# Two attentions and a gated MLP in one kernel: the fourfold pooled sum of the stacked head pairs is split between ScalarE and VectorE, the fp32 v loads get a third buffer, and the written order of all steps is drawn anew

## The chip, the core and the metric

The kernel runs on one core of one Trainium2 chip. The core has a matrix engine (TensorE, PE in the profile, with its weight loads as PEld), VectorE (DVE), ScalarE (ACT), GpSimd (POOL) and SyncE (SP), which only issues transfers; 16 DMA engines move data. Each engine has its own queue of instructions and works it off in order; semaphores make it wait for the others. The metric is the device time of one execution in microseconds, as the median of several runs.

## What is computed

For q, k and v of 8 batches, 8 heads, 576 positions and 64 features, two attentions are added: one over keys and queries averaged in fours, whose result is repeated fourfold, and a local one, in which a position sees only those less than four away. The sum, laid out as 4608 tokens of 512 features, goes through a gated MLP.

```python
q_d = q.reshape(B, H, Sd, 4, D).mean(axis=3)          # k_d, v_d alike
out_up = np.repeat(sm_attn(q_d, k_d, v_d), 4, axis=2)
mask = np.abs(pos[:, None] - pos[None, :]) < 4
out_local = softmax(where(mask, scale * q @ k.T, -1e9)) @ v
x = (out_up + out_local).transpose(0, 2, 1, 3).reshape(4608, 512)
return (np.maximum(x @ w_gate, 0) * (x @ w_val)) @ w_out   # 512 -> 1536 -> 512
```

## The kernel before, in words

**Work and tiles.** The heads are taken two at a time, 32 pairs, and the tokens in nine chunks of 512. Each pair leaves its part of x, transposed (features on partitions), in `xT`. As soon as four pairs have filled the columns of a chunk, the chunk's MLP can run: `hg` and `hv` (L919) are its products with w_gate and w_val, `gate` the gated product on VectorE, and then follow the products with w_out. Many of the large products are computed by a scheme that needs seven half-sized products in place of eight (classes `Unit`, `Half7`, `Seven`; L1004, L1264, L1167), with additions on VectorE and copies out of PSUM on ScalarE (L1275, L1280, L1178, L1185).

**Pairs.** Pairs 0 to 11 go through an older form. For the first nine, q and k are turned by TensorE (`tr`, L540 and L556), taken out of PSUM by ScalarE and VectorE (`ev`, L576 and L579), scored (`s1`), exponentiated on ScalarE (`ex`, `ed`) and masked on VectorE (`ma`). v is pooled by TensorE (`vd`, L618) and copied out by ScalarE (`vc`). For the first four pairs `sd`, `su` and `xp` make the output and turn it into `xT`. Between them, `warm` and `brief` issue matmuls on zeros, whose results nobody reads.

Pairs 12 to 31 are "stacked": the two heads of a pair lie in the two halves of the partitions, and one step, `so` (`emit_section`, L852), interleaves the matmuls of three pairs' phases (scores of the next pair, denominators of this one, numerators of the last). ScalarE exponentiates (L858, L863) and makes the reciprocals as exp(-ln(x)) (L874, L877). VectorE multiplies (`xn`, L880) into one buffer, `xn`, of 576 local and 144 pooled columns. Then `xsum` (L886, VectorE) adds the local columns and the pooled ones, each of which it reads four times in a row by a step of zero, and writes the pair's 128x576 part of `xT`.

**v of the stacked pairs** comes twice. One load, in fp16 and by GpSimd's queue, serves the local attention (`v`). The other, in fp32 and by SyncE's queue, serves the pooled one (`v4`, `emit_load_v4`). GpSimd folds the latter's twelve rows in two steps: `v2` (L589) adds rows in twos from buffer `v4n[hp % 2]` into `v2full[hp % 2]`, and `v1` (L597) adds again into `vp[hp % 3]`, in fp16.

**Order.** All instructions stand in the order of the string `SEQ`, step by step; each engine gets its own instructions in that order. POOL issues the loads of q, k, v (L454, L459, L504, L477) and of the weights (L1076, L1082) and does the folds; SP issues the first q load, the transposes by DMA (`flip`), the fp32 v loads and the outputs. `SEQ` begins with `cast`, `ones/6`, `ones/4`, `ones/5` (L1504: three memsets of `vw` buffers on POOL) and `loadk/0`. Ahead of `SEQ` stand the first q load, three loads of constants and twelve wide filler matmuls.

Of the kernel before, what the change touches and what calls it, by code (L numbers as in the profile page):

```python
# [23 lines left out]
loadk/3 ev/2/01A/0 xp/0/0/4 ev/2/11A/2 ev/2/00A/0 xe/0/1V/5 s1/2/0 vc/1/6 sd/1/6 ma/1/1 rd/1/6 xe/0/0A/4 td/1/6 wv/0
wg/0 warm/3/7 su/1/4 loadk/4 ex/2/1/0 vd/2/6 ed/2/0 ex/2/0/0 tr/3/1/2 tr/3/2/3 vc/2/6 edge/1 wg/1 ru/1/4 tr/3/0/0
tu/1/0/4 tu/1/1/4 ev/3/21V/3 ev/3/11A/2 ev/3/10A/2 ev/3/01A/0 ev/3/00A/0 sd/2/6 xp/1/0/4 ev/3/20V/3 loadq/5 ma/2/0
xe/1/0A/4 xp/1/1/5 rd/2/6 s1/3/0 ma/2/1 loadk/5 ex/3/0/0 xe/1/1V/5 loadk/6 hv/0/0/7 loadv/4 su/2/4 td/2/6 ed/3/0
loadv/5 vd/3/6 ru/2/4 warm/4/1 tu/2/1/4 hv/1/0/1 ex/3/1/0 tu/2/0/4 tr/4/0/0 xp/2/0/4 ma/3/1 vc/3/6 ev/4/00A/0 loadq/6
# [5 lines left out]
hg/3/*/0 wo/2 wo/3 ev/5/10A/3 hg/2/*/6 den/4/1/5 gate/0/7 gate/1/1 den/4/0/4 relu/3/0 qk/b3/0@0 tr/6/1/0 relu/2/6
loadv/8 hv/2/*/7 vd/5/1 num/4/1/3 qk/a2/1@0 ln/4 gate/2/7 ev/6/10A/0 inv qk/b0/0@0 num/4/0/2 s1/5/4 vc/5/1 hv/3/*/1
xn/2 ex/5/0/4 hg/4/*/2 ed/5/4 ev/6/11V/0 xsum/4 qk/a0/1@0 gate/3/1 tr/7/1/0 tr/6/0/4 tr/6/2/1 qk/b2/0@0 ex/5/1/4
ma/5/1 ev/6/20V/1 hv/4/*/3 ev/7/10V/0 hg/5/*/6 ev/7/11V/0 ev/6/21V/1 relu/4/2 ev/6/00A/4 vd/6/1 ev/6/01V/4 den/5/1/5
ma/5/0 qk/b1/0@0 flip/9 vc/6/1 gate/4/3 den/5/0/4 ln/4 num/5/0/2 num/5/1/3 relu/5/6 hv/5/*/7 inv hg/7/*/1 qk/a1/1@0
gate/5/7 relu/7/1 v/a/1@0 s1/6/4 ed/6/4 xn/2 v/b/0@0 ex/6/1/4 hv/8/*/0 v4/b/1@0 ex/6/0/4 ma/6/1 qk/a3/1@0 qk/b0/1@0
hv/7/*/3 sum/2/0@1 hg/8/*/2 relu/8/2 hg/6/*/7 tr/7/2/1 ma/6/0 tr/7/0/6 relu/6/7 gate/7/3 den/6/0/4 ev/7/00A/6 gate/8/0  # L40
ev/7/21A/1 edge/0 ev/7/20A/1 den/6/1/5 num/6/1/3 v4/a/0@1 qk/b1/0@2 tr/8/2/0 ln/4 xsum/5 ev/7/01V/6 num/6/0/2 v2/b/0@1
qk/b3/1@0 qk/b2/1@0 ev/8/21A/0 inv hv/6/*/7 gate/6/7 hv/9/*/1 ev/8/20A/0 s1/7/4 ed/7/4 ex/7/1/4 qk/b1/0@1 ex/7/0/4
hg/9/*/0 relu/9/0 xn/2 hg/10/*/3 qk/a1/0@1 hg/11/*/7 flip/10 hv/10/*/6 zs/0.1/0@1 ma/7/1 vd/7/4 ma/7/0 hv/11/*/0
relu/10/3 den/7/1/5 gate/9/1 xsum/6 vc/7/4 tr/8/0/1 relu/11/7 p/1/0@1 wt/0 keep/1/0@1 gate/10/6 gate/11/0 ev/8/01A/1
num/7/0/6 den/7/0/4 next/0/1@0 qk/a3/0@1 ln/4 num/7/1/7 tr/8/1/0 sumhi/0/0@1 qk/b1/1@0 p/2/0@1 qk/b0/0@1 next/1/1@0
ev/8/00A/1 wt/1 p/5/0@1 inv ev/8/10A/0 sumhi/1/0@1 wt/2 ev/8/11A/0 xn/6 p/6/0@1 xsum/7 flip/11 v/b/1@0 keep/2/0@1
vd/8/5 wt/3 zs/0.0/0@1 vc/8/5 qk/b2/0@1 p/7/0@1 scores/a/0@1 hg/0/0@1 exp/a0/0@1 keep/3/0@1 ed/a/0@1 qk/a2/0@1
mask/a0/0@1 hv/0/0@1 p/4/0@1 qk/b3/0@1 qk/a0/0@1 exp/a1/0@1 o/a10/0@1 mask/a1/0@1 v2/a/1@1 relu/0/0@1 o/a00/0@1
sum/3/0@1 c22//0@1 c11//0@1 o/a01/0@1 c21//0@1 qk/a1/1@1 o/a11/0@1 hg/1/0@1 hg/2/0@1 ln/a/0@1 next/0/0@1 inv/a/0@1
v4/b/0@1 relu/1/0@1 const p/3/0@1 hg/3/0@1 relu/2/0@1 xn/a/0@1 v1/a/1@1 gate/0/0@1 c12//0@1 hv/2/0@1 xsum/a/0@1 vd/9/7  # L50
pool/b/0@1 qk/a0/1@1 hv/1/0@1 flip/12 relu/3/0@1 gate/2/0@1 vd/10/2 gate/1/0@1 vc/9/7 scores/b/0@1 hg/4/0@1 exp/b0/0@1
exp/b1/0@1 qk/b2/0@2 qk/a2/1@1 next/1/0@1 flip/13 hv/3/0@1 relu/4/0@1 ed/b/0@1 hv/4/0@1 vc/10/2 p/1/1@1 mask/b1/0@1
mask/b0/0@1 gate/3/0@1 pool/a/0@1 o/b01/0@1 tn/1/0@1 keep/1/1@1 o/b10/0@1 o/b00/0@1 gate/4/0@1 o/b11/0@1 zs/1.1/0@1
v/a/0@1 ln/b/0@1 p/6/1@1 v/b/0@1 qk/a3/1@1 inv/b/0@1 hg/5/0@1 qk/b1/1@1 xn/b/0@1 relu/5/0@1 hv/5/0@1 keep/2/1@1
next/2/0@1 scores/a/1@1 exp/a1/1@1 xsum/b/0@1 next/3/0@1 p/2/1@1 p/7/1@1 keep/3/1@1 flip/14 exp/a0/1@1 hg/0/1@1
ed/a/1@1 gate/5/0@1 hv/0/1@1 p/5/1@1 zs/3.1/0@1 mask/a1/1@1 qk/b0/1@1 o/a01/1@1 relu/0/1@1 mask/a0/1@1 o/a10/1@1
zs/1.0/0@1 o/a00/1@1 c11//1@1 o/a11/1@1 ln/a/1@1 inv/a/1@1 p/4/1@1 c22//1@1 qk/a1/1@2 p/3/1@1 c21//1@1 hg/2/1@1
pool/b/1@1 gate/0/1@1 c12//1@1 qk/b2/1@1 relu/2/1@1 xn/a/1@1 qk/b3/1@1 hv/2/1@1 gate/2/1@1 scores/b/1@1 hv/1/1@1
v/a/1@1 zs/2.1/0@1 exp/b0/1@1 exp/b1/1@1 mask/b0/1@1 hg/1/1@1 qk/a1/0@2 mask/b1/1@1 ed/b/1@1 xsum/a/1@1 o/b00/1@1
pool/a/1@1 o/b01/1@1 ln/b/1@1 relu/1/1@1 xq/0/0@2 gate/1/1@1 o/b10/1@1 inv/b/1@1 o/b11/1@1 v2/b/1@1 hg/4/1@1  # L60
so/b400/1@1 xn/b/1@1 hv/4/1@1 hg/3/1@1 qk/a0/0@2 pool/b/0@2 relu/4/1@1 gate/4/1@1 xsum/b/1@1 ed/a4/0@2 v4/b/1@1
hv/3/1@1 qk/a2/0@2 sq/4.23.0.1/0@2 exp/a4/0@2 relu/3/1@1 so/a460/0@2 sk/4.23.0.1/0@2 tn/3/0@1 v1/a/0@2 hg/5/1@1
v1/b/1@1 ln/a6/0@2 gate/3/1@1 next/0/1@1 relu/5/1@1 sq/4.23.0.5/0@2 sq/0.70.2.1/0@2 ed/b4/0@2 sq/4.23.0.2/0@2 flip/15
sum/2/0@2 zs/2.0/0@1 exp/b4/0@2 sk/4.23.0.5/0@2 hv/5/1@1 xq/1/0@2 vh/10.6/0@2 sk/0.70.2.1/0@2 sq/4.23.0.6/0@2
zs/3.0/0@1 sq/0.70.2.6/0@2 sk/4.23.0.2/0@2 xq/2/0@2 xq/3/0@2 gate/5/1@1 up/54.1/0@2 next/1/1@1 sumhi/0/0@2
sk/0.70.2.2/0@2 sq/4.23.0.7/0@2 sf/4.23.0.11/0@2 uk/54.1/0@2 sq/0.70.2.2/0@2 qk/b0/0@2 sumhi/1/0@2 sq/4.23.0.3/0@2
sq/0.70.2.7/0@2 sf/4.23.0.22/0@2 sf/4.23.0.12/0@2 up/54.6/0@2 sq/0.70.2.5/0@2 uk/54.2/0@2 vh/4.1/0@2 sq/4.23.0.4/0@2
sk/0.70.2.5/0@2 sf/0.70.2.22/0@2 up/54.5/0@2 up/54.7/0@2 inv/a/0@2 sf/4.23.0.21/0@2 v4/a/1@1 qk/a0/1@2 sq/0.70.2.4/0@2
uk/54.5/0@2 sf/0.70.2.21/0@2 qk/a2/0@3 sum/3/0@2 qk/a3/0@2 up/54.3/0@2 gt/4.1.0/0@2 gt/10.6.1/0@2 uf/54.22/0@2
sf/0.70.2.11/0@2 v2/b/0@2 up/54.2/0@2 uf/54.11/0@2 pool/a/0@2 up/54.4/0@2 uf/54.12/0@2 so/b163/0@2 qk/b3/0@2  # L70
uf/54.21/0@2 sq/0.70.2.3/0@2 v/b/0@2 sf/0.70.2.12/0@2 ln/b6/0@2 sq/1.50.0.1/0@2 vh/0.7/0@2 after/3/0@2 ed/a1/1@2
qk/a1/0@3 sk/1.50.0.1/0@2 flip/16 inv/b/0@2 sq/1.50.0.6/0@2 xn/a3/0@2 sk/1.50.0.2/0@2 vh/6.6/0@2 sq/1.50.0.5/0@2
v2/a/0@2 sk/1.50.0.5/0@2 next/2/0@2 exp/a1/1@2 gt/0.7.2/0@2 v1/a/1@2 v/b/1@1 sq/1.50.0.3/0@2 gt/6.6.3/0@2
sq/1.50.0.2/0@2 sq/2.32.0.1/1@2 sq/1.50.0.7/0@2 qk/a3/0@3 vh/1.7/0@2 sf/1.50.0.12/0@2 sf/1.50.0.11/0@2 sk/2.32.0.1/1@2
sq/2.32.0.5/1@2 v4/b/0@2 v1/b/0@2 sf/1.50.0.22/0@2 sq/1.50.0.4/0@2 flip/17 pool/b/1@2 sq/2.32.0.2/1@2 gt/1.7.0/0@2
v4/a/0@2 sf/1.50.0.21/0@2 sq/2.32.0.6/1@2 sk/2.32.0.2/1@2 so/a406/1@2 sq/2.32.0.3/1@2 sq/2.32.0.7/1@2 ln/a0/1@2
xsum/a/0@2 sf/2.32.0.11/1@2 vh/7.1/0@2 next/0/0@2 vh/2.0/1@2 exp/b4/1@2 xn/b6/0@2 qk/a3/1@2 ed/b4/1@2 gt/7.1.1/0@2
# [1502 lines left out]
```

## Time and profile before

| | before |
|---|---|
| median of 3 runs | 336.67 us (336.05 to 337.72) |
| profiled execution, its own time | 339.31 us |
| its span, first to last instruction | 337.5 us |
| mean granted TensorE clock | 0.990 |
| HBM read / written | 46.53 MB / 9.44 MB |
| POOL's transfers (software queue) | 116800 packets, 19.51 MB |

The page gives the busy time of each engine over the span, and digits for 40 equal slices (9 is 90% or more of the slice; the clock's digits are tenths of full speed). Groups have a line of the kernel, an engine, an operation, what is written and read, the count, the busy time in us, the mean ns of one, and the idle time of the engine ahead of them with what ended it. A wait is put down to what ended it last. The chain of waits follows the work that ended last back to the start. A row of a timeline begins with its start and duration in us. Matmuls are pipelined, so a group of them is shorter than the sum of its members. Names of buffers are shared: `vw`, `qk` and others hold different things in the course of the kernel.

### The profile page before, as it was taken

The page shows a single profiled execution, that of the slowest core. Times are in us where ns is not written, and L with a number is a line of the kernel's source. Part 1 is how long each engine was busy: PE and PEld are TensorE (multiplying, and loading weights), DVE is VectorE, ACT ScalarE, POOL GpSimd, SP SyncE. Part 2 cuts the span into 40 slices and gives each one's busy share as a digit, 9 for nine tenths or more (in the row PEclk, how much of TensorE's full clock was granted, in tenths as well). Part 3 has the DMA queues.
Part 4 walks back from the last instruction along what each step waited for, and adds up shares of the span by engine and source line. Part 5 has one row for each costly group of instructions (what it writes and reads, how often), then busy time and mean ns, then how long its engine had stood idle before and what let it go on. Part 6 is the DMA issues. An engine that isn't in the chain of part 4 may idle for free.

```text
span 337.5 us, 10448 instructions
## 1 busy us (share of the span) xinstructions
PE 328.8 (97%) x4176; PEld 237.9 (70%) x4176; DVE 284.4 (84%) x551; ACT 223.9 (66%) x553; POOL 182.4 (54%) x252
## 2 busy tenths in 40 slices
...
PEclk9959999999999999999999999999999999999999
...
GB/s 125 158 195 168 194 193 158 164 138 221 141 192 140 178 149 188 149 173 114 117 223 181 154 180 110 157 171 138 117 38 2 3 96 47 2 47 18 50 94 124
DMA packets 154966, 43.94 MB, mean 130 GB/s; under 512 B 139725, under 2 KB 149621, under 8 KB 154917
## 3 DMA queue, kind: packets, MB, share of 16 engines
q0 software_dynamic: 116800, 19.51, 78.5%
...
q14 instruction: 18, 0.14, 0.2%
q10 hardware_dynamic: 112, 0.04, 0.1%
HBM read 46.53 MB, written 9.44 MB: 166 GB/s over the span
## 4 chain that ended last, share of the span: by engine, by line
PE 87%; DVE 5%; POOL 3%; DMA 2%; issue 1%; ACT 1%; DVEq 0%; POOLq 0%
PE ps L919 28%; PE ps L1264 25%; PE ps L1167 18%; PE ps L852 6%; PE ps L1004 3%; DMA vw<-in_v_dram 2%; POOL qk L454 2%; DVE gT L1359 1%; PE ps L540 1%; PE ps L618 1%; DVE xT L1250 1%; DVE xo L998 1%; POOL vw L504 1%; PE ps L738 1%; PE ps L648 1%
## 5 line engine op out<-in xcount | busy, mean ns | idle before, releaser
L919 PE MATMUL ps<-xT,wv_sb 128*128 128x512 f16 x352 | 89.9, 380 | 0.0
L919 PEld LDWEIGHTS <-wv_sb 128*128 128x128 f16 x352 | 33.6, 98 | 27.4
L1275 ACT COPY ps<-ps 128x256 f32<-128x256 f32 x80 | 28.5, 365 | 19.6 <-PE ps L1264 16.5
L1264 PE MATMUL ps<-xT,qk 128*128 128x256 f16 x240 | 40.2, 273 | 0.2 <-DVE xT L1250 0.2
L1359 DVE SCALAR_TENSOR_TENSOR gT<-r,ps 128x512 f16<-128x512 f16 x55 | 37.2, 680 | 3.6 <-PE ps L919 2.6
L589 POOL TENSOR_TENSOR v<-v 112x384 f32<-112x384 f32 (+1 forms) x21 | 22.7, 1079 | 22.5 <-DMA v<-in_v_dram 22.0
L1264 PE MATMUL ps<-xT,wg_sb 128*128 128x256 f16 x180 | 31.4, 273 | 0.3 <-DVE r L1282 0.3
L1280 ACT CAST r<-ps 128x256 f16<-128x256 f32 x55 | 20.5, 376 | 16.6 <-PE ps L1264 12.0
L527 DVE TENSOR_REDUCE qkd<-qkT 128x288 f16<-128x1152 f16 x23 | 30.8, 1341 | 0.0
L1264 PEld LDWEIGHTS <-qk 128*128 128x128 f16 x240 | 22.7, 98 | 10.0 <-DVE xT L1250 0.4
L477 POOL DMA_DIRECT2D vw<-in_v_dram x40 | 29.0, 736 | 0.4 <-issue 0.2
L597 POOL TENSOR_TENSOR vd<-v 48x192 f16<-48x192 f32 x40 | 25.7, 642 | 5.8 <-PE ps L852 3.7
L919 PE MATMUL ps<-xT,wg_sb 128*128 128x512 f16 x104 | 26.3, 380 | 0.0
L1264 PEld LDWEIGHTS <-xo 128*128 128x128 f16 x240 | 23.1, 98 | 4.3 <-DVE xo L998 0.4
L1178 ACT COPY ps<-ps 128x256 f32<-128x256 f32 x54 | 19.2, 367 | 8.4 <-PE ps L1167 6.0
L459 POOL DMA_DIRECT2D qk<-in_q_dram x28 | 20.6, 736 | 7.7 <-PE ps L768 3.9
L1264 PE MATMUL ps<-wt,xo 128*128 128x256 f16 x180 | 23.9, 273 | 0.1
L459 POOL DMA_DIRECT2D qk<-in_k_dram x28 | 20.6, 739 | 2.7 <-DMA wg_sb<-in_moe_w_gate_dram 1.0
L1264 PEld LDWEIGHTS <-wg_sb 128*128 128x128 f16 x180 | 17.4, 98 | 6.7 <-issue 0.3
L931 DVE TENSOR_TENSOR gT<-r,ps 128x512 f16<-128x512 f16 x24 | 16.1, 679 | 5.9 <-PE ps L919 5.6
L1282 DVE TENSOR_TENSOR r<-ps,xT 128x256 f16<-128x256 f32 x44 | 17.5, 417 | 3.6 <-PE ps L1264 2.4
L1264 PEld LDWEIGHTS <-gT 128*128 128x128 f16 x180 | 17.4, 98 | 3.7 <-DVE gT L1359 0.9
(176 smaller groups left out, 862.8 us busy)
## 6 DMA issues: line engine op xcount, KB each, us to landing
...
vw<-in_v_dram POOLq DMA_DIRECT2D x12, 168.0 KB, 7.5
...
```

The lines of the kernel that those rows point to most:

```text
L459: nc.gpsimd.dma_start(dst.rearrange("p (j h d) -> p j h d", h=2, d=64)[:, :, hh, :], _dap(src, off + (1 - hh if hp >= NEW else hh) * S * D ...
L477: nc.gpsimd.dma_start(t[lo : lo + 64, j0:j1], _dap(v, base + j0 * QB * D, [[D, 64], [QB * D, j1 - j0], [1, D]]),)
L527: nc.vector.tensor_reduce(out=qkd[hp % 2].rearrange("p i t -> p (i t)"), in_=qkT[hp % 4][:, 0 : 2 * S].rearrange("p (t f) -> p t f", f=4), ...
L589: nc.gpsimd.tensor_tensor(out=m, in0=t[:, :, 0:128], in1=t[:, :, 128:256], op=ALU.add)
L597: nc.gpsimd.tensor_tensor(out=vp[hp % 3][lo : lo + 48, :, lo : lo + 64], in0=m[:, :, 0:64], in1=m[:, :, 64:128], op=ALU.add)
L852: nc.tensor.matmul(out=out, lhsT=left, rhs=right, start=zone not in begun, stop=True, skip_group_check=True)
L919: nc.tensor.matmul(out=out, lhsT=w[:, kk, bass.ts(jj, 128)], rhs=xT[:, kk, c * TCH : (c + 1) * TCH], start=(kk == 0), stop=(kk == 3),)
L1167: nc.tensor.matmul(out=out, lhsT=self.left[i][t], rhs=self.right[i][t], start=(i == 1 and t == 0), stop=(t == n - 1), skip_group_check=True,)
L1264: nc.tensor.matmul(out=out, lhsT=self.left[i - 1][k], rhs=self.right[i - 1][k], start=(i == 1 and k == 0), stop=(k == n - 1), skip_group_c ...
L1275: nc.scalar.copy(out=o, in_=x)
L1280: nc.scalar.copy(out=o, in_=self.d if i == 11 else self.a)
L1359: lambda c, jj, b, t: nc.vector.scalar_tensor_tensor(out=gT[c % 2][:, jj, :], in0=tg[t], scalar=0.0, in1=ps[:, b, :], op0=ALU.max, op1=ALU ...
```

## The change

The pooled half of the stacked pairs' sum gets a step of its own, `xe`, on ScalarE: it writes the pooled columns fourfold into the pair's part of `xT`. `xsum` then adds the local columns to what is there.

```diff
-    def emit_xsum_st(hp):
-        b = hp // NPB
-        nc.vector.tensor_tensor(
-            out=xT[:, hp % NPB, b * S : (b + 1) * S].rearrange("p (t f) -> p t f", f=4),
-            in0=xn_st[:, 0:S].rearrange("p (t f) -> p t f", f=4),
-            in1=_sap(xn, (0, 128), S, [[1, SD], [0, 4]]),
-            op=ALU.add,
-        )
+    def x_cols(hp):
+        b = hp // NPB
+        return xT[:, hp % NPB, b * S : (b + 1) * S]
+
+    def emit_expand(hp):
+        nc.scalar.copy(
+            out=x_cols(hp).rearrange("p (t f) -> p t f", f=4), in_=_sap(xn, (0, 128), S, [[1, SD], [0, 4]])
+        )
+
+    def emit_xsum_st(hp):
+        nc.vector.tensor_tensor(out=x_cols(hp), in0=xn_st[:, 0:S], in1=x_cols(hp), op=ALU.add)
...
         "xn": lambda hp, a: emit_xn_st(hp, int(a)),
+        "xe": lambda hp, a: emit_expand(hp),
         "xsum": lambda hp, a: emit_xsum_st(hp),
```

The fp32 v loads rotate over three buffers, the third in the room of the old `v2full`, and the first fold is written in place.

```diff
-    v2full = ring(2, [128, 4, 128], FP32, "v2_")
+    v2big = keep.tile([128, 1024], FP32, name="v2")
+    v2full = [v2big[:, 512 * i : 512 * (i + 1)].rearrange("p (a b) -> p a b", b=128) for i in range(2)]
+    v4n.append(v2big[:, 0:768])
...
-                    v4n[hp % 2][lo : lo + n], _dap(v, off + hh * S * D, [[12 * D, n], [1, 12 * D]])
+                    v4n[hp % 3][lo : lo + n], _dap(v, off + hh * S * D, [[12 * D, n], [1, 12 * D]])
...
-                t, m = v4n[hp % 2][0:WK].rearrange("p (w x) -> p w x", w=3), v2full[hp % 2][0:WK, 0:3]
+                t = v4n[hp % 3][0:WK].rearrange("p (w x) -> p w x", w=3)
+                m = t[:, :, 0:128]
...
-                m = v2full[hp % 2][lo : lo + 48, 0:3]
+                m = v4n[hp % 3].rearrange("p (w x) -> p w x", w=3)[lo : lo + 48]
```

`SEQ` is written anew. It has the old steps and twenty `xe`, the same matmuls among them, in another order, and several steps use other PSUM banks. Its beginning:

```diff
-cast ones/6 ones/4 ones/5 loadk/0 tr/0/0/2 ev/0/01A/2 pads ev/0/00A/2 tr/0/1/3 tr/0/2/4 ev/0/21V/4 ev/0/10A/3 loadq/1
-ev/0/11A/3 loadk/1 ev/0/20V/4 tr/1/0/7 ev/1/01A/7 s1/0/2 ev/1/00A/7 tr/1/1/0 tr/1/2/1 ex/0/0/2 brief/16/2 ev/1/11A/0
-loadv/0 ex/0/1/2 ma/0/0 loadq/2 ev/1/20V/1 ev/1/10A/0 vd/0/6 ev/1/21V/1 warm/5/6 ed/0/2 ma/0/1 s1/1/0 loadk/2 vc/0/6
-su/0/4 ex/1/1/0 warm/2/7 loadv/1 ru/0/4 sd/0/6 tu/0/1/4 warm/5/7 rd/0/6 td/0/6 ed/1/0 tu/0/0/4 tr/2/1/2 loadq/3
...
+cast tr/0/0/2 ev/0/00A/2 loadk/0 loadv/0 pads tr/0/1/3 ev/0/10A/3 ev/0/11A/3 tr/0/2/4 vd/0/6 ev/0/01A/2 loadq/1
+loadk/1 loadk/3 ev/0/21V/4 loadv/1 tr/1/0/7 ev/0/20V/4 s1/0/2 loadq/2 loadk/2 vc/0/6 ev/1/00A/7 tr/1/2/1 tr/1/1/0
+ev/1/01A/7 loadv/2 loadv/3 ed/0/2 warm/5/6 sd/0/6 loadq/3 loadk/4 wv/0 loadq/4 ex/0/0/2 brief/16/2 ev/1/21V/1
+ev/1/20V/1 wg/0 loadk/5 ev/1/10A/0 loadv/4 rd/0/6 ma/0/0 ev/1/11A/0 loadk/6 s1/1/0 loadq/5 td/0/6 ex/0/1/2 ma/0/1
+warm/2/7 ex/1/0/0 ma/1/0 su/0/4 ru/0/4 ed/1/0 vd/1/6 tr/2/0/0 ex/1/1/0 tr/2/2/3 tu/0/1/4 tu/0/0/4 tr/2/1/2 vc/1/6
+ev/2/21V/3 ev/2/20V/3 ev/2/01A/0 ev/2/00A/0 ma/1/1 ev/2/11A/2 xp/0/1/5 xp/0/0/4 sd/1/6 xe/0/1V/5 ev/2/10A/2 s1/2/0
+xe/0/0A/4 ex/2/0/0 ed/2/0 su/1/4 rd/1/6 td/1/6 warm/5/7 warm/1/7 vd/2/6 tr/3/0/0 ex/2/1/0 ma/2/0 ru/1/4 tu/1/1/4
```

In POOL's queue the head then reads: loadk/0, loadv/0, loadq/1, loadk/1, loadk/3, loadv/1, loadq/2, loadk/2, loadv/2, loadv/3, loadq/3, loadk/4, wv/0, loadq/4, wg/0 and so on (before: ones three times, loadk/0, loadq/1, loadk/1, loadv/0, loadq/2, loadk/2, loadv/1, loadq/3, loadv/3, loadq/4, loadv/2, loadk/3, wv/0, wg/0). `ones/6` now follows loadv/7, `ones/4` follows wo/2, and `ones/5` stands among the loads for the fourteenth pair and later. On TensorE `vd/0` stands ahead of the second pair's `tr`, and the fillers `warm/5/7` and `warm/1/7` ahead of `vd/2`; the first `hv` (L919) stands behind `vd/3`. In the stage of the stacked pairs an `xe` stands between each pair's `xn` and its `xsum`, with other steps between them.

More of the change, by code (lines that the diff above doesn't have):

```diff
@@ L24 @@
[L24 to L28, printed above, removed]
@@ L34 @@
[L34 to L38, printed above, removed]
@@ L39 @@
[L39 to L77, printed above, removed]
-sk/2.32.0.5/1@2 qk/b1/0@3 qk/a0/0@3 v2/b/1@2 sq/3.51.1.1/1@2 qk/b0/1@2 sf/2.32.0.22/1@2 up/74.1/1@2 qk/a2/1@2
@@ new lines @@
+tr/4/2/3 tr/4/1/2 td/3/6 ev/4/11A/2 ev/4/10A/2 loadv/7 ru/3/4 tu/3/0/4 tu/3/1/4 hg/0/0/6 hg/0/1/6 hv/0/2/7 hg/1/0/0
+wv/3 ones/6 ev/4/21V/3 loadq/8 ev/4/20V/3 wg/3 xp/3/1/5 xp/3/0/4 hv/1/2/1 hg/0/2/6 wo/1 xe/3/1V/5 wo/0 wo/2 xe/3/0A/4
+s1/4/2 ex/4/0/2 hg/0/3/6 relu/0/6 hv/1/3/1 hv/0/3/7 hg/1/1/0 hg/1/2/0 hg/1/3/0 vd/4/6 ed/4/2 tr/5/0/2 tr/5/1/3
+ex/4/1/2 tr/5/2/4 ev/5/01A/2 relu/1/0 vc/4/6 ev/5/10A/3 ev/5/11A/3 ev/5/00A/2 gate/0/7 ma/4/0 ma/4/1 hv/2/*/7 hg/2/*/6
+relu/2/6 ev/5/20V/4 ev/5/21V/4 gate/1/1 den/4/1/5 den/4/0/4 ln/4 inv gate/2/7 num/4/1/3 num/4/0/2 xn/2 vd/5/1 hg/3/*/0
@@ new lines @@
+vc/5/1 s1/5/4 ex/5/0/4 hv/3/*/1 ex/5/1/4 ed/5/4 hg/4/*/2 hg/5/*/6 relu/3/0 relu/4/2 hv/4/*/3 ma/5/0 ma/5/1 tr/6/0/4
+gate/3/1 xsum/4 gate/4/3 relu/5/6 tr/6/1/0 ev/6/00A/4 ev/6/11V/0 ev/6/01V/4 ones/4 num/5/0/2 den/5/1/5 tr/6/2/1
+ev/6/10A/0 wo/3 num/5/1/3 qk/b1/0@0 den/5/0/4 const v4/a/0@1 ln/4 ev/6/21V/1 ev/6/20V/1 hv/5/*/7 gate/5/7 inv vd/6/1
+tr/7/1/0 xn/2 vc/6/1 loadv/8 ev/7/10V/0 s1/6/4 hg/7/*/1 qk/b3/0@0 ed/6/4 qk/b2/0@0 qk/a1/0@1 qk/b0/0@0 hg/8/*/2
+v/b/0@0 ev/7/11V/0 qk/a0/1@0 ex/6/1/4 hv/8/*/0 v/a/1@0 hg/6/*/7 relu/8/2 ma/6/1 qk/a3/1@0 relu/7/1 qk/a2/1@0 ex/6/0/4
```

358 lines of the change are left out of this document (198 added, 160 removed).

## The prediction

> **What bounds the kernel now.** I read the page first, then the engines by stretches, then the waits, the timelines of the first 26 us and the chain.
>
> ```profile
> span 337.5 us, 10448 instructions
> PE 328.8 (97%) x4176; PEld 237.9 (70%) x4176; DVE 284.4 (84%) x551; ACT 223.9 (66%) x553; POOL 182.4 (54%) x252
> PEclk9959999999999999999999999999999999999999
> ```
>
> TensorE (PE) works 328.8 of 337.5 us, and the change adds and removes no matmul. So it can only win what PE loses: idle time, and time at a low clock. The third fortieth of the span (16.9 to 25.3 us; the 5 in the clock row) ran at little more than half clock. In the stretches (columns: length, PE, PE's weight loads, DVE, ACT, POOL busy, granted clock, DMA share, GB/s):
>
> ```profile
> 5.00:10.00 5.00, 3.62 (x76) 2.46 (x74) 1.76 (x9) 2.63 (x10) 5.00 (x7) 1.00 1.60 136
> 15.00:20.00 5.00, 3.50 (x67) 3.00 (x67) 2.87 (x9) 3.11 (x9) 3.44 (x5) 0.84 1.68 190
> 20.00:25.00 5.00, 5.00 (x63) 3.96 (x60) 3.03 (x9) 3.19 (x8) 2.90 (x4) 0.50 1.50 190
> 130.00:160.00 30.00, 29.69 (x463) 21.99 (x456) 27.93 (x51) 20.85 (x52) 20.43 (x29) 1.00 1.46 158
> 160.00:190.00 30.00, 29.78 (x403) 21.68 (x401) 27.18 (x48) 18.82 (x47) 24.96 (x36) 1.00 1.47 176
> 190.00:220.00 30.00, 29.23 (x451) 20.81 (x450) 29.06 (x50) 20.75 (x51) 24.50 (x34) 1.00 1.38 145
> ```
>
> Two places lose: the head, and the stage of the stacked pairs from 130 to 220 us, where PE idles 0.31 + 0.22 + 0.77 = 1.30 us and VectorE (DVE) is 91 to 97% busy. PE's own waits name them:
>
> ```profile
> PE ps L618 <- DMA vw<-in_v_dram: 1.5, 1, 1.5
> PE ps L540 <- DMA qk<-in_q_dram: 1.2, 1, 1.2
> PE ps L1264 <- DVE r L1282: 0.3, 1, 0.3
> ```
>
> Both head waits are for loads that GpSimd's queue (POOL) issues. PE's timeline there (start, duration):
>
> ```profile
> 5.68 1.21 PE L540 MATMUL ps<-gT,qk 96*64 96x144 f16 x24
> 8.05 0.44 PE L540 MATMUL ps<-gT,qk 96*64 96x144 f16 x8 [1.16 <-DMA qk<-in_q_dram]
> 11.79 0.54 PE L697 MATMUL ps<-vw,att 112*128 112x65 f16 x12
> 13.25 0.94 PE L540 MATMUL ps<-gT,qk 96*64 96x144 f16 x24
> 14.12 0.51 PE L618 MATMUL ps<-vw,cst_sb 112*128 112x128 f16 x6
> 18.29 0.71 PE L618 MATMUL ps<-vw,cst_sb 112*128 112x128 f16 x6 [1.50 <-DMA vw<-in_v_dram]
> 18.93 1.65 PE L540 MATMUL ps<-gT,qk 96*64 96x144 f16 x24
> 23.29 0.87 PE L697 MATMUL ps<-vw,att 112*128 112x65 f16 x12
> 23.97 0.83 PE L618 MATMUL ps<-vw,cst_sb 112*128 112x128 f16 x6
> ```
>
> The wait of 1.50 us ends at 18.29 and the half clock follows it: the same 24, 12 and 6 matmuls take 1.65, 0.87 and 0.83 us where they took 0.94, 0.54 and 0.51 before, together 3.35 against 1.99. From 18.29 to 25.3 us, 7.0 us long, PE has no further wait, so the low clock costs about 7.0 x (1 - 1.99/3.35) = 2.8 us. The head thus loses 1.16 + 1.50 + 2.84 = 5.5 us. (What PE does ahead of 5.68, where the first row stands, are twelve fillers; they stay.)
>
> The loads come late because POOL starts late and is then always busy:
>
> ```profile
> 0.74 2.08 POOL L1504 MEMSET vw<- 112x768 f16 x3 [0.29 <-POOLq L1564]
> 2.77 0.91 POOL L454 DMA_DIRECT2D qk<-in_k_dram  x1
> 10.76 1.00 POOL L504 DMA_DIRECT2D vw<-in_v_dram  x1
> 12.40 0.86 POOL L1076 DMA_DIRECT2D wv_sb<-in_moe_w_val_dram  x1
> vw<-in_v_dram POOLq DMA_DIRECT2D x1, 168.0 KB, 7.5
> wv_sb<-in_moe_w_val_dram POOLq DMA_DIRECT2D x1, 384.0 KB, 8.6
> ```
>
> (The last two rows are the DMA view narrowed to the issues at 10.76 and 12.40; the last number is the time to landing.) The load that PE waits for at 18.29 was the eleventh issued, at 10.76, and landed 7.5 us later.
>
> **The change, part by part: the order in the head.** The new order takes the three memsets of ones from the front of POOL's queue to behind later loads, so the first load can be issued at about 0.74 instead of 2.77: 2.0 us earlier, and all behind it. loadv/2, which ended the wait at 18.29, becomes the ninth load. From the first issue at 2.77 to the thirteenth at 12.40 lie twelve steps, 0.80 us each, so it is issued at 0.74 + 8 x 0.80 = 7.1 and lands, 7.5 us later, at 14.6 instead of 18.3. Its matmuls (vd/2) keep their place behind su/1, so that wait should go, and with it the low clock. loadv/0 comes second, and vd/0 ahead of the second pair's transposes, so that work that is there covers the wait of 1.16. The first slice of w_val stays thirteenth and lands at 21.0 - 2.0 = 19.0; the new order asks for it only behind vd/3, which ended at 23.97 + 0.83 = 24.8 before, so supply allows 5.8 us. Next late is ScalarE (ACT), which evacuates and exponentiates for each pair in turn:
>
> ```profile
> 6.16:25.30 19.14, 13.66 (x34) 0.82 1.72 171
> 4.18 0.83 ACT L1498 CAST qk<-q 96x768 f16<-96x768 f32 x1 [2.17 <-DMA q<-in_q_dram]
> ```
>
> (First row: ACT's own work in that stretch, 13.66 of 19.14 us. Second: the cast of the first q block, in ACT's timeline.) Even without a pause it saves at most 5.5 us. PE's own 5.5 is the same size. Low end: the shift of the queue alone, 2.0. I take 4.0, a little over the middle, because both long waits have named causes that go, while each pair still hands work to and fro between PE, ACT and DVE. The memsets, moved, cost POOL the same 2.08 us later, beside PE at full work. The loads now share the DMA engines with the first q load on the sync queue, which ended the wait ahead of the cast at 4.18. The cast is done at 5.01, the fillers at 5.68, so 0.67 us of delay is hidden; beyond that it costs PE one for one, which I leave to rival 4.
>
> **The expansion and the sum.** The old sum reads the pooled part with a step of zero:
>
> ```profile
> L886 DVE TENSOR_TENSOR xT<-xn x20: 744/751/1493, 116.1 to 262.7; 128x576 f16<-128x576 f16 x20
> L1152 DVE TENSOR_TENSOR xT<-xT 128x512 f16<-128x512 f16 x8 | 3.3, 417 | 0.0
> L1250 DVE TENSOR_TENSOR xT<-xT 128x512 f16<-128x512 f16 x20 | 10.5, 535 | 0.0
> L858 ACT ACTIVATE att<-ps 128x576 f16<-128x576 f32 x20 | 13.2, 660 | 0.0
> L1275 ACT COPY ps<-ps 128x256 f32<-128x256 f32 x80 | 28.5, 365 | 19.6 <-PE ps L1264 16.5
> 193.73 1.41 DVE xT L886
> 166.99 0.80 DVE xT L886
> ```
>
> The new sum reads both operands and writes in unit steps, like the 128x512 subtractions, 417 ns undisturbed and 535 on average beside GpSimd. Scaled to 576 elements: 0.47 to 0.60 us against a median of 0.75. Twenty times the difference is 3.0 to 5.6 us of DVE; I take 5, nearer the undisturbed row, because the old sum's median stands close to its minimum. Of this only what lies on the chain counts: two of the twenty sums are there (the last two rows), and PE's idle in the stage is 1.30 us in all. I take 0.8 of it; the other end is 0, if DVE's next step is late anyway.
>
> [...]
>
> The added copy on ACT has no row. The exponential of the same 128x576 takes 660 ns, a 128x256 copy 365: I take 0.66, with bounds of 0.37 (that copy is narrower) and 0.82 (that copy scaled by its elements). That is 20 x 0.66 = 13.2 us on ACT, which is 62 to 70% busy in the stage. It is free as long as ACT's pauses hold it: before its 80 L1275 copies alone ACT idles 19.6 us, 16.5 of them waiting for PE. Uncovered it delays the PSUM copies queued behind it, and PE waits for these (second rival). The sum now waits for ACT as well; behind it on DVE stand the gates, on which PE's second matmuls wait. The order puts a few steps between the two.
>
> **The third v buffer.**
>
> ```profile
> L589 POOL TENSOR_TENSOR v<-v 112x384 f32<-112x384 f32 x20 | 20.9, 1046 | 20.0 <-DMA v<-in_v_dram 19.5
> ```
>
> The folds cost the same in place. Up to 20.0 us of POOL's waiting for the fp32 loads can go; a buffer is now held through the second fold too, which takes some of it back. No wait of PE names POOL or a DMA after 18.29, so I book 0; if that cover is gone, a late fold holds one section of the attention, some tenths of a us. The loads are issued on SP earlier, ahead of transposes that wait behind them if the buffer isn't free: also 0.
>
> **Sum.** Against the profiled span: 337.5 - 4.0 - 0.8 = 332.7. The profiled execution took 339.31, 1.8 around its span; the timed runs' median, 336.67, lies 0.8 below the span. The same gain of 4.8 from the median gives **331.9 us**. Bounds: nothing below 5.5 + 1.3 = 6.8, so 329.9; at the low end 2.0 + 0, so 334.7.
>
> **Rivals.** (1) *Supply alone*: the head follows the loads and everything moves by 2.0 us, the stage gives nothing: 334.7. For it: the DMA share is above 1 throughout the head. Against: loadv/2 moves 3.7 us, not 2.0.
>
> (2) *ACT becomes the bound (slower)*: expansions stand directly ahead of PSUM copies. A copy has on average 19.6/80 = 0.25 us of idle ahead of it, so an expansion there delays it by 0.41; if PE waits each time, 20 x 0.41 = 8.2 us, and 336.7 - 4.0 + 8.2 = 340.9. It makes the kernel slower by over 0.5% from (4.0 + 1.7)/20 = 0.28 us a piece. Against: PE has no wait on ACT in its list, and the order was drawn with the copies in it.
>
> (3) *The low clock comes again*: the cause is not the wait but the thin head (3.62 and 3.50 us of PE in two stretches of 5), and another pause brings it back: the forecast loses 2.8, 334.7. For it: the timeline shows only that one followed the other. [...]
>
> (4) *The head gains nothing*: earlier loads delay the first q load by as much as they win (the row of its cast, above), or a new order of evacuations brings new waits: 336, no change.
>
> **How the numbers follow.** Forecast 0.56, its own range 329.9 to 334.4; supply 0.13, clock 0.12, ACT 0.10, nothing 0.09. A measurement of this kernel tells about 0.5% (1.7 us) from no change. Rivals 1 and 3, at 334.7, are just over that: 0.20 of their 0.25 counts as faster, 0.05 as the same. Faster 0.76, same 0.05 + 0.09 = 0.14, slower 0.10. The range 329.9 to 336.2 leaves out rival 2, half of rival 4 and a tail below, some 0.2.
>
> **What would show it.** Right: no 5 in the clock row; the first POOL load before 1 us; no DMA in PE's list with over 0.5 us; the first gate/value matmuls (L919) back to back some 4 us earlier; the sum at 0.47 to 0.60 us; the new copy near 0.66 us. Wrong: the clock row still with a 5, PE waits on L1275 or L1280 in the stage, a PE idle above 1.30 us between 130 and 220, or a head whose L919 starts less than 2 us earlier.

## The result, and the profile after

The changed kernel takes **334.25 us** (median of six executions, 334.06 to 334.60) against 336.50 us for the kernel before (336.05 to 337.72, and one execution of 666.18 that the ratio leaves out). The ratio is **0.9916, 95% interval 0.9893 to 0.9940**: faster, by 2.25 us in the medians and by 2.8 us (2.0 to 3.6) if the ratio is taken of 336.50, where 4.8 was forecast. The profiled executions, however, are 5.0 us apart: spans of 337.5 and 332.5 us. The difference between 5.0 and 2.25 is the main thing to be explained.

The page of the changed kernel: the span, the busy times and the clock row.

```profile
span 332.5 us, 10464 instructions
PE 326.1 (98%) x4176; PEld 236.0 (71%) x4176; DVE 281.2 (85%) x551; ACT 233.1 (70%) x573; POOL 181.9 (55%) x252
PEclk9999999999999999999999999999999999999999
```

The 5 has left the clock row. DVE has lost 3.2 us, ACT has gained 9.2. TensorE's list of waits holds a single DMA now, of 0.4 us, and no wait on ACT:

```profile
PE ps L1271 <- DVE r L1289: 0.4, 1, 0.4
PE ps L543 <- DMA qk<-in_q_dram: 0.4, 1, 0.4
PE ps L1271 <- DVE y_sb L1289: 0.4, 1, 0.4
```

(Lines have moved by 3 to 7: L543, L622, L926, L1271, L1282 of the new kernel are L540, L618, L919, L1264, L1275 of the old.) The timeline of the head, first POOL, then ACT, then TensorE:

```profile
1.31 0.90 POOL L457 DMA_DIRECT2D qk<-in_k_dram  x1 [0.86 <-POOLq L1572]
10.93 0.86 POOL L1083 DMA_DIRECT2D wv_sb<-in_moe_w_val_dram  x1
```
```profile
4.36 0.83 ACT L1506 CAST qk<-q 96x768 f16<-96x768 f32 x1 [2.34 <-DMA q<-in_q_dram]
```
```profile
7.97 0.44 PE L543 MATMUL ps<-gT,qk 96*64 96x144 f16 x8 [0.36 <-DMA qk<-in_q_dram]
16.23 0.50 PE L622 MATMUL ps<-vw,cst_sb 112*128 112x128 f16 x6
16.66 0.94 PE L543 MATMUL ps<-gT,qk 96*64 96x144 f16 x24
19.59 0.50 PE L622 MATMUL ps<-vw,cst_sb 112*128 112x128 f16 x6
19.93 0.60 PE L926 MATMUL ps<-xT,wv_sb 128*128 128x512 f16 x2
```

The first matmul of the MLP before, for comparison with the last row:

```profile
22.89 0.61 PE L919 MATMUL ps<-xT,wv_sb 128*128 128x512 f16 x1
```

The first load is issued at 1.31, not at 2.77: 1.46 us earlier, and so is the slice of w_val (10.93 for 12.40). The third pair's `vd` (L622 at 16.23) starts 2.1 us earlier with no wait ahead of it, and the same 24 transposes behind it take 0.94 us, not 1.65. The fourth pair's stands at 19.59 instead of 23.97, 4.4 us earlier. The cast of the first q block ends 0.18 us later, at 5.19, still ahead of the fillers' end. Measured at the fourth pair's `vd`, the head gave 4.4 of the 5.0 us between the two profiled executions. The first matmul of the MLP moved less, by 3.0 us (22.89 to 19.93), because the new order puts it behind the fourth pair's `vd`.

The stage of the stacked pairs, in stretches (columns as in the prediction), of after and then, for the two stretches not shown yet, of before:

```profile
60.00:100.00 40.00, 39.65 (x452) 24.49 (x450) 38.09 (x63) 26.04 (x51) 33.44 (x47) 1.00 1.74 171
100.00:130.00 30.00, 29.65 (x456) 21.17 (x455) 26.61 (x47) 22.34 (x54) 22.41 (x33) 1.00 1.34 167
130.00:160.00 30.00, 29.61 (x405) 22.01 (x403) 27.28 (x49) 21.62 (x54) 27.59 (x39) 1.00 1.99 146
160.00:190.00 30.00, 29.83 (x405) 21.93 (x402) 25.61 (x49) 20.69 (x52) 19.93 (x28) 1.00 1.43 170
190.00:220.00 30.00, 29.85 (x455) 21.20 (x453) 27.94 (x50) 23.41 (x56) 19.29 (x30) 1.00 1.45 172
```
```profile
60.00:100.00 40.00, 39.88 (x497) 25.25 (x498) 37.48 (x61) 27.87 (x54) 32.71 (x47) 1.00 1.76 170
100.00:130.00 30.00, 30.00 (x409) 21.81 (x410) 26.82 (x47) 20.43 (x52) 21.90 (x31) 1.00 1.58 158
```

Between 130 and 220 us TensorE's idle fell from 1.30 to 0.39 + 0.17 + 0.15 = 0.71 us, but between 60 and 130 it rose from 0.12 to 0.70. Over the whole stage it is 1.41 us after and 1.42 before: between these two executions the stage gave nothing. Yet the costs of the single instructions came out nearly as forecast (groups of after, then the old sum's of before: busy, mean ns, idle ahead of them):

```profile
L893 ACT COPY xT<-xn 128x576 f16<-128x576 f16 x20 | 13.6, 682 | 1.6 <-DVE xn L884 1.5
L898 DVE TENSOR_TENSOR xT<-xn,xT 128x576 f16<-128x576 f16 x20 | 11.6, 582 | 0.7 <-ACT xT L893 0.5
L593 POOL TENSOR_TENSOR v<-v 112x384 f32<-112x384 f32 x20 | 20.9, 1045 | 24.0 <-DMA v<-in_v_dram 23.5
```
```profile
L886 DVE TENSOR_TENSOR xT<-xn 128x576 f16<-128x576 f16 x20 | 16.4, 820 | 0.1
```

The expansion takes 682 ns. The sum takes 582 where the old one took 820 on average, and it waits for ACT 0.5 us in all. GpSimd's first fold is as long as before, and its waiting for the fp32 loads is 23.5 us, not less than the 19.5 of before. These means are those of one execution: a second one of the changed kernel has 484 ns for the same sums (below).

### The profile page after: what moved, and what is told of

Read it like the earlier page. It is cut to its first block, busy times and chain, and to the rows that moved or that the text cites. A ratio compares the mean times of both kernels' runs of the same rounds, so it can differ in the third digit from the quotient of the medians.

```text
span 332.5 us, 10464 instructions
## 1 busy us (share of the span) xinstructions
PE 326.1 (98%) x4176; PEld 236.0 (71%) x4176; DVE 281.2 (85%) x551; ACT 233.1 (70%) x573; POOL 181.9 (55%) x252
## 4 chain that ended last, share of the span: by engine, by line
PE 87%; DVE 7%; issue 2%; DMA 2%; POOL 1%; ACT 1%; DVEq 0%; POOLq 0%
PE ps L926 27%; PE ps L1271 24%; PE ps L1174 18%; PE ps L856 7%; PE ps L1011 3%; DVE xo L1005 2%; DMA qk<-in_k_dram 2%; PE ps L543 1%; DVE gT L1366 1%; PE ps L622 1%; PE ps L742 1%; DVE xT L1257 1%; DVE qkd L530 1%; PE ps L641 1%; PE ps L652 1%
## 5 line engine op out<-in xcount | busy, mean ns | idle before, releaser
L926 PE MATMUL ps<-xT,wv_sb 128*128 128x512 f16 x352 | 90.0, 379 | 0.0
L926 PEld LDWEIGHTS <-wv_sb 128*128 128x128 f16 x352 | 33.5, 98 | 26.5
L1271 PE MATMUL ps<-xT,qk 128*128 128x256 f16 x240 | 41.0, 273 | 0.0
L1282 ACT COPY ps<-ps 128x256 f32<-128x256 f32 x80 | 28.3, 367 | 14.8 <-PE ps L1271 14.5
L593 POOL TENSOR_TENSOR v<-v 112x384 f32<-112x384 f32 (+1 forms) x21 | 22.0, 1050 | 24.0 <-DMA v<-in_v_dram 23.5
L1271 PE MATMUL ps<-xT,wg_sb 128*128 128x256 f16 x180 | 32.5, 273 | 0.6 <-DVE r L1289 0.4
L1271 PEld LDWEIGHTS <-qk 128*128 128x128 f16 x240 | 23.0, 98 | 9.4 <-DVE qk L1150 0.4
L1271 PEld LDWEIGHTS <-xo 128*128 128x128 f16 x240 | 23.1, 98 | 4.8 <-DVE xo L1005 0.8
L926 PE MATMUL ps<-xT,wg_sb 128*128 128x512 f16 x104 | 26.4, 380 | 0.0
L1271 PE MATMUL ps<-wt,xo 128*128 128x256 f16 x180 | 24.4, 273 | 0.4 <-DVE xo L1005 0.2
L1271 PEld LDWEIGHTS <-wg_sb 128*128 128x128 f16 x180 | 17.0, 98 | 9.0 <-issue 1.4
L1271 PEld LDWEIGHTS <-gT 128*128 128x128 f16 x180 | 17.4, 98 | 3.4 <-issue 0.5
```

Of the source, the lines that this page charges most:

```text
L593: nc.gpsimd.tensor_tensor(out=m, in0=t[:, :, 0:128], in1=t[:, :, 128:256], op=ALU.add)
L926: nc.tensor.matmul(out=out, lhsT=w[:, kk, bass.ts(jj, 128)], rhs=xT[:, kk, c * TCH : (c + 1) * TCH], start=(kk == 0), stop=(kk == 3),)
L1271: nc.tensor.matmul(out=out, lhsT=self.left[i - 1][k], rhs=self.right[i - 1][k], start=(i == 1 and k == 0), stop=(k == n - 1), skip_group_c ...
L1282: nc.scalar.copy(out=o, in_=x)
```

## The experiments

Two theories stood against each other. **Head**: the gain comes from POOL's queue in the head, chiefly from the three memsets; the split sum and the third buffer are no gain by themselves. **Split**: the lighter sum is a good part of it. And a question ran beside them: how much of the 5.0 us is the low clock, and does every execution of before have it?

**The kernel before, again** (no edit).

> The kernel before, unchanged. Theory H (head): the profiled execution of before, 337.5 us of span at clock 0.990, had a low clock in the head that most executions don't have. Then most spans here lie near 337.5 - 2.8 = 334.7 us at a clock near 1.000, and at most a few near 337.5 at 0.990. Theory E (every run has the low clock): all spans near 334.5 to 337.5 with a clock of 0.990.

Measured: 337.12 us (336.42 to 338.88 in 12 executions), ratio 1.0006 [0.9982, 1.0029]. Its profiled execution has a span of 334.6 us, 2.9 less than the first one, with the same program. The page and TensorE's waits:

```profile
PEclk9999999999999999999999999999999999999999
```
```profile
PE ps L540 <- DMA qk<-in_k_dram: 0.7, 1, 0.7
PE ps L618 <- DMA vw<-in_v_dram: 0.6, 1, 0.6
PE ps L540 <- DMA qk<-in_q_dram: 0.6, 1, 0.6
```

There is no 5, and the waits for loads are 0.7, 0.6 and 0.6 where they were 1.5 and 1.2. In the 72 executions of the kernel before that these studies hold, the mean clock is 0.988 to 0.990 in four (median 338.98 us), 0.994 to 0.995 in seven, and 0.998 or more in 61 (median 336.74). The low clock of the first profile was thus one execution in eighteen, at 2.2 us apiece, and the median hardly contains it.

**Only the memsets moved late**, in the old order:

```diff
-cast ones/6 ones/4 ones/5 loadk/0
+cast loadk/0
...
+loadv/7 ones/6
...
+wo/2 ones/4 wo/3 ones/5
```

> The kernel before with the three memsets of ones moved behind later loads in GpSimd's queue, as in the new order, and nothing else. Theory H: the loads are issued 1.4 to 2.0 us earlier, the wait of 1.50 us ahead of 18.29 shrinks below 0.5, and the time falls by 1.3 to 2.0 us, to about 334.8. Theory S (the gain is made in the stage of the stacked pairs by the split sum): 336.3 to 336.7, as before.

Measured: 334.92 us (333.92 to 337.24), ratio 0.9950 [0.9924, 0.9976]: faster by 0.50%, and 1.73 us under the 336.65 of the kernel before on that chip. The first load is issued at 1.31, as in the changed kernel. One part of the expectation failed: the wait for loadv/2 is still 0.70 us there, where the execution of before just shown has 0.63. What shrank are the two waits ahead of it, from 0.6 and 0.7 to 0.2 us and none. The interval overlaps that of the whole change, so whether the rest of the new order adds to the memsets' 0.50% isn't settled by the times.

**Only the memsets moved back**, in the new kernel:

```diff
-cast tr/0/0/2
+cast ones/6 ones/4 ones/5 tr/0/0/2
```

> The changed kernel with the three memsets of ones back at the front of GpSimd's queue, and nothing else. Theory H: the head loses 1.3 to 2.0 us again, 335.6 to 336.2. Theory S: no change, 334.3.

Measured: 336.58 us (333.87 to 339.62), ratio 0.9971 [0.9946, 0.9996]: some 0.55% more than the whole change leaves. The low clock came in 7 of its 12 executions (0.989 to 0.995). Its profiled execution, in TensorE's waits and in two stretches:

```profile
PE ps L622 <- DMA vw<-in_v_dram: 1.4, 1, 1.4
```
```profile
5.00:10.00 5.00, 2.47 (x41) 1.51 (x39) 1.49 (x8) 1.71 (x6) 5.00 (x7) 1.00 1.61 138
10.00:15.00 5.00, 5.00 (x89) 4.29 (x86) 1.98 (x6) 3.40 (x9) 5.00 (x8) 0.66 2.20 167
```

The new order asks for loadv/0 early; with the memsets ahead of it the load comes late, TensorE does 2.47 us of work in a stretch of 5, and the clock falls to 0.66 in the next. By the ratios the memsets are worth 0.50% taken out of the old order and 0.55% put into the new one. The two figures are not the same effect, though: the seven executions with the low clock have a median of 336.81 us, the other five one of 335.42. Against the 334.25 of the changed kernel, about half of the 2.3 us that the memsets cost in the new order is the clock. What one stretch holds shows where the rest comes from. The first 25 us of before (again), of before with late memsets, and of after:

```profile
0.00:25.00 25.00, 21.66 (x356) 15.06 (x356) 17.44 (x59) 16.44 (x38) 20.82 (x30) 1.00 1.47 161
```
```profile
0.00:25.00 25.00, 22.74 (x372) 15.89 (x373) 18.84 (x63) 17.09 (x41) 19.33 (x28) 1.00 1.58 169
```
```profile
0.00:25.00 25.00, 23.23 (x377) 16.51 (x378) 19.16 (x63) 16.78 (x41) 20.50 (x30) 1.00 1.64 168
```

TensorE idles 3.34, 2.26 and 1.77 us. Between these executions, all at full clock, the new head is worth 1.57 us, and the memsets alone give 1.08. The remaining 0.49 is no more than executions differ by: the second profile of the changed kernel (below) idles 2.41 us in the same stretch, which makes the new head worth 0.93.

**The old sum in the new order** (the twenty `xe` of the stacked pairs left out):

```diff
-        nc.vector.tensor_tensor(out=x_cols(hp), in0=xn_st[:, 0:S], in1=x_cols(hp), op=ALU.add)
+        nc.vector.tensor_tensor(
+            out=x_cols(hp).rearrange("p (t f) -> p t f", f=4),
+            in0=xn_st[:, 0:S].rearrange("p (t f) -> p t f", f=4),
+            in1=_sap(xn, (0, 128), S, [[1, SD], [0, 4]]),
+            op=ALU.add,
+        )
```

> The changed kernel without the twenty expansions on ScalarE, with the old sum (pooled part read by a step of zero) in the place of the new one; order otherwise the new one. Theory S: loses most of the gain, 336 or more. Theory H: within 0.5 us of 334.3; VectorE busy 4 to 5 us more, ScalarE 13 us less. Rival A (ScalarE's copies delay PE): faster than 334.3 by over 0.5 us.

Measured: 335.07 us (333.97 to 336.23), ratio 0.9944 [0.9920, 0.9969], between the two theories. VectorE is busy 2.8 us more (284.0 for 281.2), not 4 to 5. The interval overlaps the whole change's, and the second run of the changed kernel was on another chip, so whether the split is worth 0.9 us or nothing isn't settled.

**The changed kernel, again**, on the chip of three runs below (the split sum in the old order, each expansion twice, two buffers):

> The changed kernel, unchanged, to have its spread and its clock on the chip of the next three. All theories: 334 to 335, clock 0.999 or 1.000 in nearly every run.

Measured: 334.22 us (333.71 to 334.84), ratio 0.9917 [0.9886, 0.9949]. The kernel before took 336.73 us on this chip. Its profiled execution has a span of 333.1 us. TensorE's waits for loads, the first 25 us, and the sums:

```profile
PE ps L543 <- DMA qk<-in_k_dram: 0.8, 1, 0.8
PE ps L622 <- DMA vw<-in_v_dram: 0.3, 1, 0.3
```
```profile
0.00:25.00 25.00, 22.59 (x368) 15.94 (x369) 18.45 (x61) 16.87 (x41) 19.56 (x28) 1.00 1.64 168
```
```profile
L898 DVE TENSOR_TENSOR xT<-xn,xT 128x576 f16<-128x576 f16 x20 | 9.7, 484 | 0.7 <-ACT xT L893 0.5
```

The waits for loads are 1.3 us in sum (with one of 0.2 for q), where the kernel before had 1.9 when run again: shorter, but not gone. And the same sum, in the same place and with the same waits, takes 484 ns here and 582 in the first profile.

**The split sum in the old order**, each expansion directly ahead of its sum:

```diff
-... ln/a0/1@2 xsum/a/0@2
+... ln/a0/1@2 xe/a/0@2 xsum/a/0@2
```

> The kernel before with the expansion on ScalarE put directly ahead of each stacked pair's sum and the new sum; order otherwise the old one. Theory H (all of the gain is in the head): no gain, 336.5 or up to 1 us more, since here ScalarE's queue has the expansion where the old order left no room for it. Theory S (the split sum makes the gain): 334.5 to 335.5.

Measured: **347.64 us** (346.96 to 348.32), ratio 1.0317 [1.0281, 1.0353]. No theory had this. The sum's group:

```profile
L895 DVE TENSOR_TENSOR xT<-xn,xT 128x576 f16<-128x576 f16 x20 | 9.7, 486 | 20.2 <-ACT xT L890 20.2
```

Each sum is 0.33 us shorter than the old 820 ns, but DVE stands 20.2 us in front of them, since the expansion is queued on ACT behind copies that wait for TensorE (16.6 us for those of L1279). TensorE in turn waits for DVE (2.8 us for L1363, 2.2 for L1286, 1.9 for L881). Two further runs ask whether the place of the expansion does this.

**The expansion directly ahead of the sum, in the new order.** There it stands 2 to 41 steps ahead of it:

```diff
-gt/7.1.1/0@3 xe/b/0@3
+gt/7.1.1/0@3
...
-qk/a2/1@4 xsum/b/0@3
+qk/a2/1@4 xe/b/0@3 xsum/b/0@3
```

> The new kernel with each of the twenty stacked expansions moved in the order to directly ahead of its sum. Theory (where the expansion stands decides: what cost 11 us in the old order was VectorE waiting, in order, for an expansion queued late behind PSUM copies): the sums wait for ScalarE, in sum 4 to 15 us of VectorE's waits, and the time rises to 336 to 341 us. Rival (the new order of all else pays for the split; the few steps between expansion and sum do nothing): within 0.7 us of 334.2, waits of the sums on ScalarE under 3 us.

Measured: 346.56 us (345.68 to 347.77), ratio 1.0266 [1.0209, 1.0322], more than either theory had. The sum's group, and what TensorE waits for:

```profile
L899 DVE TENSOR_TENSOR xT<-xn,xT 128x576 f16<-128x576 f16 x20 | 9.8, 490 | 18.3 <-ACT xT L894 18.2
```
```profile
PE ps L1272 <- DVE xn L885: 3.2, 4, 1.3
PE ps L927 <- DVE r L1290: 2.5, 1, 2.5
PE ps L1272 <- DVE r L1290: 1.7, 4, 0.7
```

Twenty steps moved by at most 41 places, nothing else: DVE's waits for the expansions go from 0.5 to 18.2 us, and 3.5% is lost against the changed kernel. The place decides.

**The expansion early, in the old order**, directly behind its multiplication:

```diff
-... xn/a3/0@2 sk/1.50.0.2/0@2
+... xn/a3/0@2 xe/a/0@2 sk/1.50.0.2/0@2
...
-... ln/a0/1@2 xe/a/0@2 xsum/a/0@2
+... ln/a0/1@2 xsum/a/0@2
```

> The old order with the split sum and each expansion directly behind its multiplication instead of directly ahead of the sum. Theory (place decides): the sums' waits for ScalarE fall from 20.2 us to under 6, and the time from 347.6 to 337 to 342 us; it stays above 336.5, since 13 us more of ScalarE have to go into pauses the old order doesn't leave. Rival (ScalarE's extra work itself delays the PSUM copies, wherever it stands): 345 us or more, and TensorE's waits on ScalarE or on sums behind it stay.

Measured: 345.71 us (345.01 to 345.90), ratio 1.0234 [1.0183, 1.0285]. Each theory got half: the sums' waits for ACT did fall, from 20.2 to 5.9 us, but the time only from 3.2% to 2.3% above the kernel before, at the rival's figure. DVE's and TensorE's waits, and the expansions' own group:

```profile
DVE xT L896 <- ACT xT L891: 5.9, 7, 1.9
```
```profile
PE ps L1269 <- ACT ps L1280: 2.9, 6, 1.4
```
```profile
L891 ACT COPY xT<-xn 128x576 f16<-128x576 f16 x20 | 13.5, 673 | 5.8 <-DVE xn L882 5.7
```

The cost changes its face: TensorE now waits for ACT's PSUM copies. Two causes are possible and not told apart: ACT's extra work, and a place that is too early, since ACT itself now stands 5.7 us waiting for the multiplications (1.5 in the changed kernel), with the copies queued behind. The place of the expansion matters in both orders; no place tried in the old order made the split pay.

**Each expansion done twice**, in the new kernel:

```diff
-        "xe": lambda hp, a: emit_expand(hp),
+        "xe": lambda hp, a: (emit_expand(hp), emit_expand(hp)),
```

> The changed kernel with every expansion on ScalarE done twice, one directly behind the other (13 us more of ScalarE, same output). Theory H (ScalarE has room): within 1 us of the changed kernel. Rival A (ScalarE at its bound): 20 x 0.28 to 20 x 0.66, that is 5 to 13 us slower.

Measured: 339.82 us (338.98 to 340.53), ratio 1.0080 [1.0051, 1.0109]: 5.6 us more than the changed kernel on the same chip, 0.28 us for each piece of 0.68, within the rival's range. TensorE's waits now name ACT, which they didn't, and the sums wait for it 4.1 us, where it was 0.5:

```profile
PE ps L1271 <- ACT ps L1282: 1.8, 6, 0.4
```
```profile
L898 DVE TENSOR_TENSOR xT<-xn,xT 128x576 f16<-128x576 f16 x20 | 11.7, 586 | 4.3 <-ACT xT L893 4.1
```

So the price holds both ways by which a longer queue on ACT reaches TensorE.

**Two buffers in the new kernel**, the fold in place kept:

```diff
-v4n[hp % 3]
+v4n[hp % 2]
```

> The changed kernel with two buffers for the fp32 v loads instead of three, the first fold still in place. Theory H: no change, within 0.5 us of the changed kernel; GpSimd's waiting for these loads (23.5 us) grows. Rival B (the third buffer is needed by the new order): slower by over 1 us, with waits of PE in the stage of the stacked pairs that end with GpSimd or a late section.

Measured: 341.68 us (341.60 to 343.52), ratio 1.0148 [1.0114, 1.0182]. GpSimd's waits and TensorE's:

```profile
POOL vd L601 <- DMA v<-in_v_dram: 12.8, 3, 7.0
```
```profile
PE ps L856 <- POOL vd L601: 3.7, 3, 2.8
```

The second folds wait 12.8 us for DMA. They have to, because with two buffers eight loads stand in this order ahead of the second fold of the pair that had their buffer, so that this fold waits for the next load and adds up another pair's v. The new order can't be run with two buffers; what a third one is worth in an order drawn for two is not shown by this.

**The third buffer and the fold in place alone, in the old order and with the old sum** (the hunks of the change on `v4n` and `v2full`).

> The old order and the old sum, with the third fp32 v buffer and the fold in place alone. Theory (the third buffer is worth nothing by itself; it is needed by the new order, which lost 7 us without it): 336.0 to 337.2 us, no difference, though GpSimd's waits for the fp32 loads fall below the 19.5 us of before. Rival a (late folds held the stage): under 335.5 us. Rival b (earlier loads hold transposes behind them on the sync queue): over 338 us.

Measured: 344.80 us (342.42 to 347.55), ratio 1.0214 [1.0138, 1.0289]. It has the same flaw: three loads stand in the old order ahead of the second fold of the pair whose buffer they take, and there part of the pooled v is another pair's. The second folds wait 18.1 us for DMA, which they did not in before. So it doesn't tell what the third buffer is worth; that stays open.

**The new kernel without the seven filler steps** (`warm` and `brief`) among the first pairs:

```diff
-ed/0/2 warm/5/6 sd/0/6
+ed/0/2 sd/0/6
...
-ex/0/0/2 brief/16/2 ev/1/21V/1
+ex/0/0/2 ev/1/21V/1
```

> The new kernel without the seven filler steps among the first pairs (the twelve wide fillers ahead of all stay). Theory 1 (the low clock follows a pause of TensorE of 1.4 us or more): the fillers stand where TensorE would pause; with pauses as long as that the low clock comes in most executions (mean granted clock under 0.996) and the time is 335 to 338 us; without such a pause the clock stays at 1.0 and the time within 0.7 us of 334.2. Theory 2 (the low clock comes from a thin head, whatever its longest pause): clock under 0.996 in most executions although no pause reaches 1.4 us.

Measured: 339.53 us (335.81 to 341.33 in 10 executions); the ratio, 1.0027 [0.9978, 1.0075], leaves out the three longest. The mean clock is 0.978 to 0.990 in all ten. Three stretches of the profiled execution:

```profile
10.00:15.00 5.00, 2.45 (x52) 1.75 (x50) 3.25 (x9) 3.66 (x10) 2.81 (x5) 0.96 1.95 184
15.00:20.00 5.00, 5.00 (x70) 4.20 (x72) 3.20 (x10) 3.06 (x7) 3.96 (x6) 0.50 1.72 184
20.00:25.00 5.00, 4.72 (x88) 3.79 (x85) 4.05 (x13) 3.97 (x12) 2.80 (x4) 0.86 1.84 180
```

TensorE works 2.45 us of 5, then the clock is 0.50. Its longest pause there is 1.36 us, 0.04 short of the bound that the expectation set between its two theories, so by its letter the run favours the thin head. The first profile of before speaks for the pause: from 5 to 10 us it holds 3.62 us of work with a longest pause of 1.16, and the clock stays at 1.00 in the next 5 us, where 3.50 us of work with a pause of 1.50 was followed by 0.50. Which of the two brings the low clock stays open. What it shows is what the fillers do: with them the changed kernel stayed at 0.999 or more in all twelve of its executions.

## Why the prediction was right, and where it was off

**The sign and the place were right.** PE could win only in its losses, and most of them lay in the head behind POOL's queue. In the profiled pair both head waits went as described (1.16 to 0.36 us, 1.50 to none), the 5 left the clock row, the fourth pair's `vd` came 4.4 us earlier (4.0 forecast), and the cover of the first q load held. Two of the named signs fell short: the first POOL load is at 1.31, not ahead of 1 us, and the first gate/value matmul 3.0 us earlier, not 4.

**The term that was mis-sized is the low clock**, and the step that failed is "the same gain of 4.8 from the median". Of the head's 5.5 us, 2.84 were low clock that the profiled execution had and 61 of 72 others did not. The two profiled executions are 5.0 us apart (4.8 forecast), the medians 2.25. That 5.0 and 4.8 are so close is partly luck: the head gave 4.4 for 4.0, the stage 0 for 0.8, and 0.6 lie in neither. The sign stood on the page: the profiled span lay 0.8 us above the median of whole times, though a time is 1.8 us longer than its span, so that execution was about 2.6 us longer than a typical one, nearly the low clock's own price. At full clock the head was worth 0.93 to 1.57 us (3.34 of idle less 2.41 or 1.77), and 336.67 less these, 335.1 to 335.7, would have been the sum. The measured 334.25 is 0.9 to 1.5 us below that; no run shows where this lies.

**Two smaller terms.** The first load moved by 1.46 us, not 2.0, because POOL's first DMA starts at 1.31, behind 0.86 us of its own queue (L1572), and not where the memsets had started. And the stage gave 0 between the profiled executions, where 0.8 was taken from bounds of 0 and 1.30: the idle went from one stretch to another. The durations were right: 0.682 us for the copy (0.66), 0.582 and 0.484 for the sum in two profiles (0.47 to 0.60). The 4.8 us of DVE in twenty (5) agree partly by luck: the forecast set out from the old sum's median, 0.751, and 4.8 is the difference of means, 0.820 and 0.582.

**Rivals.** The time is that of rivals 1 and 3 (334.7). Rival 1 (supply alone) comes nearest in the medians: the memsets' move alone gave 334.92 us, and the stage gave nothing; against it, loadv/2's wait did go in the new order, and the DMA share is above 1 only from 5 us on (1.50 to 2.01 in the stretches up to 25 us), at 0.48 ahead of that. Rival 3's event did not come: the clock stayed at 0.999 or more. Its ground, the thin head, is neither shown nor refuted: the clock fell after stretches of 5 us with 2.45 and 2.47 us of TensorE's work, but each of them also holds a pause of 1.36 or 1.41 us. The clock differs between executions of one program: 11 executions in 72, 7 in 12 and 10 in 10 of three kernels are at 0.995 or less. The start differs too: the twelve fillers ahead of all end at 5.75 us in the first profile of before and at 6.08 in the second. What lowers the clock in one execution and not in another is not shown. Rival 2 did not happen, but its price was of the right size: ACT twice loaded costs 0.28 us a piece for 0.41, and 5.6 us in all against 8.2, a part of it by late sums and not by late copies. What was overlooked is this other door: an expansion queued late holds VectorE and costs 11 to 12 us in both orders. The sentence that the order "puts a few steps between the two" named the place on which everything hung and gave it no price.

**The third buffer** was booked at 0 and the time doesn't speak against it, but the argument that GpSimd's waiting would shrink failed (23.5 us after, 19.5 before).
